# The last chunk of the first modulation weights, loaded as two halves on two DMA queues

## Chip, cores, metric

One core of one Trainium2 chip. The metric is device time in microseconds (us) of one execution. Beside it each execution has a span, from the first to the last instruction of the core, and the mean clock that TensorE was granted. The time is some 1.8 us longer than the span. The landing of a transfer is the moment at which the last of the 16 counts on its semaphore arrives; a ring is the part of a queue that one DMA engine works through.

## The reference, cut to what matters

```python
mod = (_silu(c) @ w_mod).reshape(c.shape[0], 6, 1, -1)       # c: 1 x 512, w_mod: 512 x 3072
sa, ca, ga, sb, cb, gb = (mod[:, 0].copy(), mod[:, 1].copy(), ...)   # cut: six rows of 512
h = _layernorm(x, axis=-1) * (1 + ca) + sa
x = x + ga * _A_ref(h, A_k_cache, A_v_cache, A_wq, A_wo)     # attention, 32 heads, window of 512 keys
h = _layernorm(x, axis=-1) * (1 + cb) + sb
x = x + gb * _B_ref(h, B_w1, B_w2)                           # two-layer relu network
```

Everything in attention needs h, and h needs sa (shift) and ca (scale), which are columns 0 to 1023 of w_mod. So the first 1 MB of w_mod, four chunks of 128 rows by 1024 columns, stands at the very head of the kernel.

## The kernel before

The chunks go alternately to ACT's and SP's queue, in 2 KB rows, each with a semaphore of its own:

```python
for i in range(2):     # x, first 512 rows, in two halves
    dma(x_sb[:, 2 * i:2 * i + 2, :], xv[:, 2 * i:2 * i + 2, :], f"xa{i}", ..., eng=ACT if i else SP)
dma(c_row[:, :], c[0].rearrange("(c p) -> c p", p=P), "c", writes=[R_c])
for i in range(DC):    # DC = 4
    load_wm01(i, (ACT, SP)[i % 2])
# cut: then on SP wq of the first two heads (two transfers), keys, wq, values

def mod_cols_mm(which, bk):                    # 32 matmuls of one column each
    for cc in range(DC):                       # chunk
        for sl in (0, 1):                      # shift half, scale half
            for c2 in range(DC):
                ...  mm(bank[bk][:, col:col + 1], wm[sl][:, cc, c2 * P:(c2 + 1) * P], sc_bf[:, cc:cc + 1], ...,
                        [R_sc, wm_res(sl, cc)], ...)     # waits for the chunk
```

On TensorE these 32 matmuls stand ahead of the transposes of normalised x (tile xn). VectorE then adds 1 to the scale (tile modc), and modc and the transposes make hT, with which the attention starts. Ahead of the 32, fifteen matmuls of ones keep TensorE busy so that it is granted its full clock.

Of the kernel before, what the change touches and what calls it, by code (L numbers as in the profile page):

```python
# [1198 lines left out]
def build_fast(nc, es, top, A_x, A_k_cache, A_v_cache, A_wq, A_wo, B_x, B_w1, B_w2, c, w_mod, out, flag):  # L1199
    P = 128  # L1200
    _, Sq, D = A_x.shape
# [10 lines left out]
    DC = D // P  # L1212
# [33 lines left out]
    wm01 = wmw[:, 0:2 * DC * D].rearrange("p (c n) -> p c n", c=DC)  # L1246
# [42 lines left out]
    ACT = kb.stream("act", sem("s_act"))  # L1289
    DVE = kb.stream("dve", sem("s_dve"))  # L1290
    POOL = kb.stream("pool", sem("s_pool"))
    SP = kb.stream("sp", sem("s_sp"))

    def dsem(key):
        if key not in kb.dma_cnt:
            kb.add_dma_sem(key, sem("d_" + key))
        return key

    def dma(out_ap, in_ap, key, reads=(), writes=(), transpose=False, eng=None):
        k = dsem(key)  # L1300
        if transpose:
            return kb.op(SP, lambda e: e.dma_start_transpose(out_ap, in_ap), reads=reads, writes=writes, dma_sem=k)
        return kb.op(eng or SP, lambda e: e.dma_start(out_ap, in_ap), reads=reads, writes=writes, dma_sem=k)  # L1303

    RL = lambda name, n: [Res(f"{name}{i}") for i in range(n)]
# [4 lines left out]
    R_acc, R_wm, R_w1, R_w2 = RL("acc", TPB), RL("wm", 6), RL("w1", FC), RL("w2", FC)  # L1310
# [6 lines left out]
    R_st, R_mv, R_rstd = RL("st", NT), RL("mv", NT), RL("rstd", NT)  # L1317
    R_h0 = RL("h0", DC)
    R_q1 = RL("q1_", 2)
    R_wmc = RL("wmc", DC)  # L1320
    R_wqa = RL("wqa", 2)
    R_nmr = Res("nmr")
    R_cf, R_m01 = Res("cf"), Res("m01")
# [27 lines left out]
    wm01v = w_mod[:, 0:2 * D].rearrange("(c p) n -> p c n", p=P)  # L1351

    def load_wm01(i, eng=None):
        dma(wm01[:, i, :], wm01v[:, i, :], f"wmc{i}", writes=[R_wmc[i]], eng=eng)

    def wm_res(sl, cc):
        return R_wmc[cc] if sl < 2 else R_wm[sl]

    def load_wo(j):
        dma(wo_sb[:, j * HQ:(j + 1) * HQ, :], wov[:, j * HQ:(j + 1) * HQ, :], f"wo{j}", writes=[R_wo[j]])  # L1360
# [66 lines left out]
    def mod_cols_mm(which, bk):  # L1427
        fs = []
        for cc in range(DC):
            for sl in (0, 1):  # L1430
                for c2 in range(DC):
                    last = sl == 1 and c2 == DC - 1 and cc == DC - 1
                    fs.append(lambda sl=sl, c2=c2, cc=cc, col=sl * DC + c2, last=last: mm(
                        bank[bk][:, col:col + 1], wm[sl][:, cc, c2 * P:(c2 + 1) * P], sc_bf[:, cc:cc + 1],
                        cc == 0 and sl == 0 and c2 == 0, last, [R_sc, wm_res(sl, cc)], [bk], last))
        return fs
# [130 lines left out]
    for i in range(DC):  # L1567
        load_wm01(i, (ACT, SP)[i % 2])
# [261 lines left out]
def bass_adaLN_cond__sliding_block_cached__dense_activation_relu__prompt_kernel(  # L1830
# [14 lines left out]
    with ExitStack() as top:  # L1845
        flag = top.enter_context(nc.sbuf_tensor("flag", [1, 8], mybir.dt.int32))
        with ExitStack() as es:
            kb, fast, cut, dma_cnt, flag_ev = build_fast(nc, es, top, *args, flag)
            sems = dict(kb.sems)
            meet = top.enter_context(nc.semaphore("s_meet"))  # L1850
# [84 lines left out]
```

## Time and profile before

| | before |
|---|---|
| time, median of 3 (560.13 to 560.22) | 560.16 us |
| span of the profiled execution | 559.0 us |
| TensorE busy | 553.9 us (99%) |
| chunk 3 in the chain of waits | 2.05 to 8.82 us |
| first hT written | 9.73 us |

The lines themselves stand in the prediction. They are to be read as one chain: only the head of the kernel waits for a transfer, everything after is TensorE's work.

### The profile page before, as it was taken

The page shows a single profiled execution, that of the slowest core. Times are in us where ns is not written, and L with a number is a line of the kernel's source. Part 1 is how long each engine was busy: PE and PEld are TensorE (multiplying, and loading weights), DVE is VectorE, ACT ScalarE, POOL GpSimd, SP SyncE. Part 2 cuts the span into 40 slices and gives each one's busy share as a digit, 9 for nine tenths or more (in the row PEclk, how much of TensorE's full clock was granted, in tenths as well). Part 3 has the DMA queues.
Part 4 walks back from the last instruction along what each step waited for, and adds up shares of the span by engine and source line. Part 5 has one row for each costly group of instructions (what it writes and reads, how often), then busy time and mean ns, then how long its engine had stood idle before and what let it go on. Part 6 is the DMA issues. An engine that isn't in the chain of part 4 may idle for free.

```text
span 559.0 us, 9759 instructions
## 1 busy us (share of the span) xinstructions
PE 553.9 (99%) x4139; PEld 316.6 (57%) x4139; DVE 254.9 (46%) x556; ACT 349.4 (63%) x455; POOL 52.7 (9%) x50
## 2 busy tenths in 40 slices
PE   8999999999999999999999999999999999999997
PEld 4665555555555555555555555555555554444444
DVE  5555555553546544335445443333354438322134
ACT  5986666666666666666666666666666644432500
POOL 2000022004400000033000000332000000000000
PEclk9999999999999999999999999999999999999999
DMA  9999763422224244353353312121123110200001
GB/s 234 296 196 185 136 166 42 114 43 73 38 41 74 39 84 106 61 130 58 96 95 57 76 40 39 39 38 38 39 39 76 39 29 0 50 28 21 21 29 48
DMA packets 113356, 42.66 MB, mean 76 GB/s; under 512 B 93976, under 2 KB 112152, under 8 KB 113304
## 3 DMA queue, kind: packets, MB, share of 16 engines
q1 hardware_dynamic: 112584, 41.08, 35.5%
q10 hardware_dynamic: 720, 0.89, 0.5%
q8 instruction: 33, 0.54, 0.4%
q14 instruction: 19, 0.16, 0.1%
HBM read 18.35 MB, written 2.10 MB: 37 GB/s over the span
## 4 chain that ended last, share of the span: by engine, by line
PE 98%; DMA 1%; SPq 0%; DVE 0%; issue 0%
PE psS L1374 29%; PE psO L1374 27%; PE psQ L1374 23%; PE psW L1374 20%; DMA wmw<-in_w_mod_dram 1%; SPq L1303 0%; PE psS L1377 0%; PE psO L1377 0%; DVE PT L1752 0%; DVE PT L1754 0%; PE psW L1377 0%
## 5 line engine op out<-in xcount | busy, mean ns | idle before, releaser
L1498 ACT ACTIVATE PT<-psS 128x1024 bf16<-128x1024 f32 x254 | 260.4, 1027 | 127.0 <-PE psS L1374 126.9
L1374 PE MATMUL psS<-qT,kT 128*128 128x512 bf16 (+1 forms) x516 | 151.8, 377 | 0.1
L1374 PEld LDWEIGHTS psO<-v,PT 128*128 128x128 bf16 x2048 | 126.6, 98 | 30.2
L1374 PE MATMUL psO<-v,PT 128*128 128x129 bf16 x2048 | 137.0, 220 | 0.0
L1374 PE MATMUL psW<-wo,oT 128*128 128x512 bf16 x512 | 130.6, 379 | 0.0
L1374 PE MATMUL psQ<-hT,wq 128*128 128x512 bf16 (+1 forms) x508 | 129.6, 377 | 0.0
L1508 DVE RECIPROCAL rinv<-psO 128x4 f32<-128x4 f32 x128 | 23.3, 182 | 225.3 <-PE psO L1374 225.3
L1509 DVE TENSOR_TENSOR o<-psO,rinv 128x512 bf16<-128x512 f32 x128 | 88.5, 691 | 4.7 <-DVE rinv L1508 0.3
L1374 PEld LDWEIGHTS psS<-qT,kT 128*128 128x128 bf16 x516 | 50.0, 98 | 58.7 <-issue 0.4
L1374 PEld LDWEIGHTS psQ<-hT,wq 128*128 128x128 bf16 x508 | 49.7, 98 | 59.0 <-ACT hT L1641 0.2
L1490 ACT ACTIVATE qT<-psQ 128x512 bf16<-128x512 f32 x125 | 73.9, 591 | 0.0
L1741 ACT ACTIVATE wq<-psS 128x512 bf16<-128x512 f32 x56 | 33.4, 597 | 49.1 <-PE psS L1374 49.1
L1374 PEld LDWEIGHTS psW<-wo,oT 128*128 128x128 bf16 x512 | 45.0, 98 | 32.9 <-DVE acc L1531 1.2
L1531 DVE TENSOR_TENSOR acc<-psW,acc 128x512 f32<-128x512 f32 x48 | 33.2, 691 | 6.7 <-PE psW L1374 6.7
L1374 PE MATMUL psO<-wmw,wq 128*128 128x512 bf16 (+1 forms) x168 | 32.9, 352 | 0.0
L1534 POOL TENSOR_TENSOR acc<-acc,gaf 128x512 f32<-128x512 f32 x12 | 15.6, 1301 | 146.9 <-DVE acc L1531 139.8
L1390 POOL TENSOR_TENSOR rstd<-rstd,cst 128x4 f32<-128x4 f32 x7 | 7.2, 1027 | 216.6 <-DVE rstd L1389 216.6
L1752 DVE TENSOR_TENSOR PT<-psO,gbf 128x512 f32<-128x512 f32 (+1 forms) x12 | 7.5, 624 | 40.4 <-PE psO L1374 40.4
L1374 PE MATMUL psS<-h2T,wmw 128*128 128x512 bf16 x112 | 25.3, 379 | 0.0
L1374 PEld LDWEIGHTS psO<-wmw,wq 128*128 128x128 bf16 x168 | 15.4, 98 | 16.5
L1374 PE MATMUL psS<-hT,wmw 128*128 128x512 bf16 x112 | 24.5, 379 | 0.0
L1384 DVE BATCH_NORM_STATS2 st<-x 128x6 f32<-128x512 bf16 x31 | 21.1, 680 | 3.7 <-DMA x<-in_A_x_dram 3.7
(93 smaller groups left out, 197.1 us busy)
## 6 DMA issues: line engine op xcount, KB each, us to landing
wo<-in_A_wo_dram SPq DMA_DIRECT2D x4, 1024.0 KB, 5.9
wq<-in_A_wq_dram SPq DMA_DIRECT2D x7, 512.0 KB, 4.5
wmw<-in_B_w_dram SPq DMA_DIRECT2D x14, 256.0 KB, 3.1
wmw<-in_w_mod_dram SPq DMA_DIRECT2D x4, 512.0 KB, 5.0
oT<-o SPq DMA_TRANSPOSE x128, 2.4
out_dram<-PT SPq DMA_DIRECT2D x15, 128.0 KB, 1.7
x<-in_A_x_dram SPq DMA_DIRECT2D x3, 512.0 KB, 4.3
v<-in_A_v_cache_dram SPq DMA_DIRECT2D x8, 128.0 KB, 4.5
```

The lines of the kernel that those rows point to most:

```text
L1374: kb.op(PE, lambda e: e.matmul(out_ap, lhsT, rhs, start=start, stop=stop), reads=reads, group_writes=[R_b[k] for k in bk], signal=signal)
L1384: kb.op(DVE, lambda e: e.bn_stats(st[:, t, :], x_sb[:, t, :]), reads=[R_x[t]], writes=[R_st[t]])
L1390: kb.op(POOL, lambda e: e.tensor_tensor(rstd[:, sl], rstd[:, sl], cst[:, 0:1].to_broadcast([P, hi - lo]), op=ALU.pow), reads=R_rstd[sl] + ...
L1490: kb.op(ACT, lambda e: e.activation(qT[u % NQT][:, :], bank[bk], ACTF.Copy), reads=[R_b[bk]], writes=[R_qT[u % NQT]])
L1498: kb.op(ACT, lambda e: e.activation(PT[u % NPT][:, pr * 2:pr * 2 + 2, :], s_ps[pr][:, :, :], ACTF.Exp, scale=scale), reads=[R_b[pr * 2], R ...
L1508: kb.op(DVE, lambda e: e.reciprocal(rinv[:, u, :], o_ps[:, :, P]), reads=[R_b[5], R_b[6]], writes=[R_rinv])
L1509: kb.op(DVE, lambda e: e.tensor_tensor(o_sb[u % NOS][:, :, :], o_ps[:, :, 0:P], rinv[:, u, :].unsqueeze(2).to_broadcast([P, TPB, P]), op=A ...
L1531: kb.op(DVE, lambda e: e.tensor_tensor(acc[:, tl, :], bank[WBK], acc[:, tl, :], op=ALU.add), reads=[R_b[WBK], R_acc[tl]], writes=[R_acc[tl]])
L1534: kb.op(eng, lambda e: e.tensor_tensor(acc[:, tl, :], acc[:, tl, :], gaf[:, :], op=ALU.mult), reads=[R_acc[tl], R_ga], writes=[R_acc[tl]])
L1741: kb.op(ACT, lambda e: e.activation(h1T[b % 2][:, fc, :], bank[bk], ACTF.Relu), reads=[R_b[bk]], writes=[R_h1[b % 2][fc]], pre=all_events( ...
L1752: kb.op(DVE, lambda e: e.tensor_tensor(yt[i][:, c0:c1], bank[bk][:, c0:c1], gbf[:, c0:c1], op=ALU.mult), reads=[R_b[bk], R_gb], writes=[R_ ...
```

## The change

Its intent: the last chunk is what the head waits for, and it comes late on SP's queue; half of it on each queue should arrive sooner. The shift columns go to ACT's queue, the scale columns to SP's, each half with its own semaphore.

```diff
-    R_wmc = RL("wmc", DC)
+    R_wmc = RL("wmc", DC + 1)
...
     def load_wm01(i, eng=None):
-        dma(wm01[:, i, :], wm01v[:, i, :], f"wmc{i}", writes=[R_wmc[i]], eng=eng)
+        if i < DC - 1:
+            dma(wm01[:, i, :], wm01v[:, i, :], f"wmc{i}", writes=[R_wmc[i]], eng=eng)
+        else:
+            for sl, eng in enumerate((ACT, SP)):
+                dma(wm01[:, i, sl * D:(sl + 1) * D], wm01v[:, i, sl * D:(sl + 1) * D], f"wmc{i + sl}", writes=[R_wmc[i + sl]], eng=eng)

     def wm_res(sl, cc):
-        return R_wmc[cc] if sl < 2 else R_wm[sl]
+        return R_wmc[cc + (sl if cc == DC - 1 else 0)] if sl < 2 else R_wm[sl]
```

## The prediction

> **What bounds the kernel now.** I read the page's chain first, then the same chain cut to the first 20 us, because the change touches only transfers that are issued in the first 3 us, then the instructions by time around the last wait, then the DMA part of the first 12 us, and last the records of single DMA packets. The page:
>
> ```profile
> PE 553.9 (99%) x4139; PEld 316.6 (57%) x4139; DVE 254.9 (46%) x556; ACT 349.4 (63%) x455; POOL 52.7 (9%) x50
> ...
> PE 98%; DMA 1%; SPq 0%; DVE 0%; issue 0%
> PE psS L1374 29%; PE psO L1374 27%; PE psQ L1374 23%; PE psW L1374 20%; DMA wmw<-in_w_mod_dram 1%; SPq L1303 0%; PE psS L1377 0%; PE psO L1377 0%; DVE PT L1752 0%; DVE PT L1754 0%; PE psW L1377 0%
> ```
>
> The kernel is bound by TensorE: of 559.0 us of span it is idle for 559.0 - 553.9 = 5.1 us, and the chain is 98% matmuls. The only transfer in the chain with a share worth printing is w_mod into tile wmw, 1%. No change to transfers can bring more than a few us of 560, so 2% (11.2 us) is out of reach upwards, and downwards it would need a new wait in the body of the kernel. The same chain over the first 20 us, in order of time (start, length, what):
>
> ```profile
> 1.65 0.36 SPq L1303
> 2.01 0.04 issue
> 2.05 6.77 DMA wmw<-in_w_mod_dram
> 8.82 0.05 issue
> 8.87 0.35 PE psQ L1374 x8
> 9.22 0.47 PE psS L1377 x8
> 9.69 0.43 PE psS L1374 x2
> ```
>
> This is the whole stake. The transfer issued at 2.05 us on the SP queue is chunk 3 of the weights (chunks 0 and 2 go on ACT's queue, 1 and 3 on SP's). It lands at 8.82 us; the eight small matmuls that use it follow, then the transposes, and from there PE work is contiguous. What chunk 3's landing moves, the end of the kernel moves, until another condition takes over. The instructions around it:
>
> ```profile
> 8.08 0.73 DVE L1395 TENSOR_SCALAR xn<-x,mv,rstd 128x512 bf16<-128x512 bf16 x2
> ...
> 8.10 0.47 PEld L1374 LDWEIGHTS psQ<-sc_bf,wmw 128*128 128x128 bf16 x16 [0.48 <-DMA wmw<-in_w_mod_dram]
> ...
> 8.86 0.27 PEld L1374 LDWEIGHTS psQ<-sc_bf,wmw 128*128 128x128 bf16 x8 [0.29 <-DMA wmw<-in_w_mod_dram]
> 8.87 0.35 PE L1374 MATMUL psQ<-sc_bf,wmw 128*128 128x1 bf16 x8 [0.21 <-DMA wmw<-in_w_mod_dram]
> ...
> 9.26 0.17 DVE L1440 TENSOR_TENSOR modc<-psQ,m 128x8 f32<-128x8 f32 x1 [0.45 <-PE psQ L1374]
> ```
>
> PE's matmul row idles only 0.21 us for chunk 3 itself, since chunks 1 and 2 arrived at about 8.1 and 8.2 us. It also shows how much could ever be won: the second tile of xn, which the next transposes need, is ready at 8.08 + 0.73 = 8.81 us. With chunk 3 at hand at 8.1 us, the transposes of that tile would start at 8.81 instead of about 9.3 us, so the ceiling of the gain is about 0.5 us.
>
> The DMA part of the first 12 us gives sizes and time from issue to landing:
>
> ```profile
> wmw<-in_w_mod_dram ACTq DMA_DIRECT2D x2, 256.0 KB, 5.4
> wmw<-in_w_mod_dram SPq DMA_DIRECT2D x2, 256.0 KB, 6.6
> ...
> wq<-in_A_wq_dram SPq DMA_DIRECT2D x2, 128.0 KB, 6.7
> ```
>
> SP's chunks take 1.2 us longer, which invites the change: ACT's queue looks less loaded. The packet records say more. The landing of each chunk is counted from 16 engines. For chunk 3, fifteen of these arrive by about 7.9 us and the last at 8.82; for chunk 1 fifteen by 6.65 and the last at 8.06. So one lagging engine sets the wait. (The records don't name the engine; I infer it from packets that start where the last one ended.) On it, 2 KB packets follow each other every 80 to 84 ns. ACT's ring ends chunk 2 there at 7.84 us, SP's ring has ended chunk 1 at 7.67 us, then the eight packets of chunk 3 run alone and end at 7.92, 8.00, 8.08, ... 8.48 us; the semaphore is seen 0.34 us later, at 8.82.
>
> **What the Trainium skill says.** "DMA: Bandwidth & Descriptors", section "Issuing engines are not separate DMA queues": transfers started by different engines end on the same 16 DMA engines and interleave, and only issue time on the sequencer is saved. The trace agrees: on the lagging engine the pitch is 80 to 84 ns whether one ring or both have work. Same page, "Queues, rings and completion order": each engine takes turns between the rings that have work. The trace agrees, SP's and ACT's 2 KB packets alternate there until 7.8 us. Same page, "Why a DMA increments its semaphore by 16 and not by 1": a wait is for all engines used, which is why the laggard counts. Nothing else that I use rests on a page.
>
> **The change, part by part.** Rows of chunk 3 are 1024 bf16, 2 KB; each half has rows of 1 KB. Removed: one 256 KB transfer on SP, 128 packets of 2 KB, eight per engine. Added: 128 KB on ACT's queue behind chunk 2 (shift columns) and 128 KB on SP's behind chunk 1 (scale columns), 256 packets of 1 KB, sixteen per engine.
> - Bytes before the end of chunk 3: the same 1.5 MB (x 512 KB, weights 1 MB) for both queues together. SP had 256 + 256 + 256 = 768 KB, ACT had the same 768 KB. The rings were even in bytes; the split gives ACT 896 and SP 640.
> - Packets: over the whole trace the median is 84 ns for 2 KB, 46 ns for 1 KB and 27 ns for 512 B. On the lagging engine chunk 3 then costs 16 x 46 = 736 ns instead of 8 x 81 = 648 ns (7.84 to 8.48): **+0.09 us**. Where 1 KB rows of wq were loaded alone at 11 to 13 us, 32 packets per engine took 1.73 us, 54 ns each, which would make it 864 ns, +0.22 us.
> - Turns: SP's ring is about two packets ahead there (7.67 against 7.84 us), so its half ends first and the 512 B packets of wq behind it take turns with the last one to three packets of ACT's half: 2 x 27 ns, **+0.05 us**.
> - Issue: ACT's queue issues one more, about 0.45 us (its two issues took 0.94 us together), starting at about 2.2 us. The activation table load moves from 2.20 to about 2.65 us; ACT idles 1.26 us before x arrives at 4.96, so this costs 0. The half on ACT is issued some 0.1 us after the half on SP; both are long before 7.8 us, so 0.
> - Matmuls: the same 32. The four shift matmuls of chunk 3 come first in program order and wait for ACT's half. If it lands last, all eight still follow it (0.35 us). If it lands first, four lie ahead of the wait, and about 0.1 us is saved. I expect ACT's half last: 0.
> - Behind it: wq for the first two heads moves little and has landed by about 9.7 us against a use at 10.4; k0 lands at about 10.3 against a use at 11.65; later transfers have more. No new wait.
> Sum: +0.09 to +0.22, plus 0.05, middle about **+0.2 us** on chunk 3's landing, carried to the end by the contiguous PE chain: 560.16 + 0.2 = about 560.3 us.
>
> **Rivals.** (1) The intended gain: ACT's ring has slack and both halves land 0.3 to 0.5 us earlier, 559.7 to 559.9 us. For it: ACT's chunks land 1.2 us sooner after issue, and on the fifteen quick engines ACT's ring is done while SP's still has much of chunk 3. Against it: the wait needs the slow engine, where the rings end chunks 1 and 2 within 0.17 us of each other and the engine is busy without a gap. (2) Fair sharing hurts more: SP's ring finishes its half early and the 256 KB of wq compete with ACT's half. If that held fully on the slow engine, as many bytes again as chunk 3 would stand ahead, 8 x 81 ns = 0.65 us: 560.8 us. Against it: there the rings are nearly level. (3) The laggard's stalls shift. Its 48 packets of 2 KB would need 48 x 83 = 4.0 us of the 6.4 us from 2.1 to 8.5, so some 2.4 us are stalls (some packets took 400 to 750 ns) whose cause I can't read. More or fewer of them move the time by 0.5 us either way, limited below by the 0.5 us ceiling. (4) A new wait in the body, for instance for wq or the keys: the slack above speaks against it; it would be 1 us at most.
>
> **Range and chances.** Rivals 1 and 2 bracket the sum: 559.7 to 560.9 us should hold it 8 times in 10. The three runs before spread 0.09 us, so noise adds little. All rivals together are below 0.3% of the time, far inside 2%; I leave 0.5% for each side beyond.
>
> **What would show it.** Right: the transfer at the head of the chain ends at 8.9 to 9.1 us, on ACT's queue; the eight matmuls follow at about 9.1; all later groups keep their counts and means. Wrong: the chunk lands before 8.7 us (rival 1), or after 9.3 us with wq landing ahead of it (rival 2), or the laggard's chunks 1 and 2, which the change leaves alone, land elsewhere than at 8.06 and 8.24 us (rival 3), or PE idles for wq or keys after 10 us (rival 4).

## The result, and the profile after

The changed kernel took 560.33 us (median of 6, 560.12 to 562.37), the kernel before 560.23 us (median of 6, 560.13 to 560.43). The ratio is 1.0007, 95% interval 0.9993 to 1.0021: the same. (A ratio is the mean time of one kernel's fast runs over that of the other's of the same rounds, so it is not quite the ratio of the medians.) The time lies on the prediction. It tests little, though: the kernel before, with medians of 560.07 to 560.36 us in its four sets of executions, lies in the predicted range too.

The profiled execution is the slowest of the six, 562.37 us. From the page of the changed kernel, its busy time and the granted clock in 40 slices:

```profile
PE 555.2 (99%) x4139; PEld 317.5 (57%) x4139; DVE 255.1 (46%) x556; ACT 349.7 (62%) x455; POOL 52.7 (9%) x50
...
PEclk8999999999999999999999999999999999999999
```

TensorE has the same 4139 matmuls and is busy 1.3 us longer; the first slice has an 8 where the kernel before has a 9. The chain of the changed kernel in its first 13 us, in order of time (start, length, what):

```profile
1.72 0.45 ACTq L1303
2.17 0.03 issue
2.20 6.49 DMA wmw<-in_w_mod_dram
8.69 0.05 issue
8.73 0.35 PE psQ L1378 x8
9.09 0.88 PE psS L1381 x8
9.96 0.85 PE psS L1378 x2
```

As predicted, the transfer at the head is now ACT's half of chunk 3. But it lands at 8.69 us, 0.13 us sooner than chunk 3 did before, and not at the predicted 8.9 to 9.1 us. What is worse comes after it: the eight transposes take 0.88 us instead of 0.47, the two matmuls after them 0.85 instead of 0.43. Busy time by stretch shows why (columns: stretch and length, busy us of each engine with counts, granted TensorE clock, DMA share, GB/s):

```profile
5.54:8.95 3.41, 2.64 (x40) 1.32 (x40) 2.98 (x12) 2.13 (x8) 2.04 (x4) 1.00 1.25 235
8.95:12.36 3.41, 3.41 (x29) 2.61 (x26) 1.87 (x7) 1.67 (x4) 0.00 (x0) 0.50 1.12 271
```

From 8.95 to 12.36 us TensorE ran at half clock (half clock means that the trace shows TensorE granted half its full clock). That, and not a transfer, made this one execution 2 us slower than the other five. It is recorded as a mean clock of 0.997; the five others have 0.999 or 1.000. So there are two things to explain: what the split does when the clock is full, and whether the split brings the half clock.

The DMA part of the first 12 us (size, then us from issue to landing) shows the two halves level:

```profile
wmw<-in_w_mod_dram ACTq DMA_DIRECT2D x2, 256.0 KB, 5.1
...
wmw<-in_w_mod_dram SPq DMA_DIRECT2D x1, 256.0 KB, 6.0
...
wmw<-in_w_mod_dram SPq DMA_DIRECT2D x1, 128.0 KB, 6.5
wmw<-in_w_mod_dram ACTq DMA_DIRECT2D x1, 128.0 KB, 6.5
```

Each half, with half the bytes, takes as long from issue to landing as the whole chunk's 6.77 us before, within 0.3 us.

### The profile page after: what moved, and what is told of

Read it like the earlier page. It is cut to its first block, busy times and chain, and to the rows that moved or that the text cites. A ratio compares the mean times of both kernels' runs of the same rounds, so it can differ in the third digit from the quotient of the medians.

```text
span 560.5 us, 9760 instructions
## 1 busy us (share of the span) xinstructions
PE 555.2 (99%) x4139; PEld 317.5 (57%) x4139; DVE 255.1 (46%) x556; ACT 349.7 (62%) x455; POOL 52.7 (9%) x50
## 4 chain that ended last, share of the span: by engine, by line
PE 98%; DMA 1%; ACTq 0%; DVE 0%; issue 0%
PE psS L1378 29%; PE psO L1378 27%; PE psQ L1378 23%; PE psW L1378 20%; DMA wmw<-in_w_mod_dram 1%; ACTq L1303 0%; PE psS L1381 0%; PE psO L1381 0%; DVE PT L1756 0%; DVE PT L1758 0%; PE psW L1381 0%
```

## The experiments

Theory A: both queues share the DMA engines, and the split moves chunk 3's landing by a tenth or two of a us. Its rival, the queue theory: ACT's queue has room that SP's lacks. Clock theory: the half-clock stretch follows a stretch in which TensorE did too little, and depends on the phase at which the clock is granted. Its rivals: it is chance alone, or the split's own cost.

Twelve kernels were run, each with six executions on a chip, beside executions of the kernel before (11 on the first chip, 12 on the second). All gave correct results, apart from the one kernel that was expected to be wrong: its error is within the tolerance. I count an execution as half clock if its mean clock is 0.997, and take the mean span of the others:

| kernel | median us | ratio, 95% interval | mean span at full clock (n) | half clock |
|---|---|---|---|---|
| before, chip 1 / chip 2 | 560.20 / 560.36 | | 558.47 (10) / 558.48 (9) | 1 of 11 / 3 of 12 |
| split, first measurement | 560.33 | 1.0007, 0.9993 to 1.0021 | 558.50 (5) | 1 of 6 |
| e1 split again (chip 1) | 560.08 | 1.0002, 0.9985 to 1.0019 | 558.20 (5) | 1 of 6 |
| e2 before again (chip 1) | 560.07 | 0.9993, 0.9981 to 1.0006 | 558.30 (6) | 0 of 6 |
| e3 halves both on SP (chip 1) | 560.20 | 0.9996, 0.9983 to 1.0008 | 558.40 (6) | 0 of 6 |
| e4 chunk 3 whole on ACT (chip 1) | 561.72 | 1.0018, 1.0001 to 1.0035 | 558.80 (3) | 3 of 6 |
| e5 chunk 3 not awaited (chip 2) | 560.40 | 0.9996, 0.9981 to 1.0011 | 558.33 (6) | 0 of 6 |
| e6 256 KB more ahead of it (chip 2) | 561.62 | 1.0015, 0.9995 to 1.0036 | 558.60 (3) | 3 of 6 |
| e7 split by partitions (chip 2) | 560.64 | 1.0005, 0.9988 to 1.0022 | 558.74 (5) | 1 of 6 |
| e8 split, queues exchanged (chip 2) | 560.41 | 0.9998, 0.9981 to 1.0015 | 558.44 (5) | 1 of 6 |
| e9 before, filled (chip 2) | 561.64 | 1.0016, 1.0001 to 1.0031 | 558.60 (6) | 0 of 6 |
| e10 as e4, filled (chip 2) | 562.09 | 1.0023, 1.0007 to 1.0038 | 558.93 (6) | 0 of 6 |
| e11 split, filled (chip 2) | 561.55 | 1.0014, 0.9998 to 1.0030 | 558.47 (6) | 0 of 6 |
| e12 as e6, filled (chip 2) | 562.19 | 1.0023, 1.0008 to 1.0038 | 559.07 (6) | 0 of 6 |

"Filled" is explained at e9. A single full-clock span of the kernel before ranges from 558.1 to 559.3 us, so differences of 0.2 us between two rows are at the edge of what these runs resolve.

**e1, the split again.** No edit.

> The changed kernel once more, unaltered. The profiled execution of the first measurement took 562.37 us, the other five 560.12 to 560.65; its trace shows TensorE's clock at half for one stretch of 3.4 us (8.95 to 12.36 us). Theory A (transfers share the engines; what the split does is a tenth or two of a us at the landing of chunk 3): median 560.2 to 560.5 us, ratio 0.9995 to 1.0010, chunk 3 lands 0.6 to 0.9 us after chunk 2. Clock theory: most executions near 560.3, and about one in six over 561.5 us, with half clock after 8 us in the trace if the profile catches one. Rival (the split itself costs 1.5 us or more): the profile shows a span of 560 us or more again with full clock.

The ratio is 1.0002, five executions took 560.00 to 560.11 us and one 562.32 us at clock 0.997, so the clock theory's one in six came out, and the split itself does not cost 1.5 us. Its profile is at full clock: the chain at the head reads

```profile
2.21 5.81 DMA wmw<-in_w_mod_dram
8.02 0.05 issue
8.06 0.35 PE psQ L1378 x8
8.41 0.54 PE psS L1381 x8
```

Chunk 3 landed at 8.02 us, 0.50 us after chunk 2, where theory A expected 0.6 to 0.9: a miss to the good side. Its transposes began earlier, but waited inside for xn (0.54 instead of 0.47 us).

**e2, the kernel before again.** No edit.

> The kernel before, unaltered, as the noise floor of both the time and the trace. All theories: ratio 0.9995 to 1.0005. Theory A: chunk 2 lands between 7.7 and 8.3 us, and chunk 3 0.5 to 0.65 us after it, wherever the lagging engine stands. Clock theory: if the half-clock stretch is a matter of phase alone, the kernel before has it too in some executions (over 561.5 us); if it is the change that opens the gap, never.

Chunk 2 landed at 8.03 us and chunk 3 at 8.55, 0.53 us after, as expected. The ratio is 0.9993, just outside the expected band: the noise floor is some 0.07%, 0.4 us. None of its six executions was at half clock, but one of the 11 executions of the kernel before beside it was (562.14 us), and three of 12 on the other chip. So the half clock is not the split's own; the split had it in 2 of 12, the kernel before in 4 of 35 (all executions together). These do not differ.

**e3, both halves on SP's queue.**

```diff
-            for sl, eng in enumerate((ACT, SP)):
+            for sl, eng in enumerate((SP, SP)):
```

> Chunk 3 in two halves of 1 KB rows, but both on SP's queue. It separates the size of the packets from the second queue. Theory A: on the slowest engine the same 16 packets of 1 KB, nothing beside them; chunk 3 lands 0.6 to 0.85 us after chunk 2, time 560.2 to 560.5 us, as the split over both queues within 0.15 us. Queue theory (ACT's ring has room that SP's has not): later than the split over both queues by 0.3 us or more.

Its last half landed 0.50 us after chunk 2 (7.72 against 7.22 us), not 0.6 to 0.85, and the time is the kernel before's. The queue theory's 0.3 us of loss did not come. The trace tells less than hoped: in this execution no engine lagged, chunk 1 was down at 6.20 us where the other profiles have 7.0 to 8.1.

**e4, chunk 3 whole on ACT's queue.**

```diff
-        load_wm01(i, (ACT, SP)[i % 2])
+        load_wm01(i, (ACT, SP, ACT, ACT)[i])
```

> Chunk 3 whole, 2 KB rows, on ACT's queue behind chunk 2; SP's next transfer is wq. Theory A: the rings are level on the slowest engine, so chunk 3 stays eight packets, but wq's 512 B packets take turns with it: landing 0.65 to 0.95 us after chunk 2, time 560.2 to 560.6 us. Queue theory: ACT's ring is ahead, so chunk 3 lands 0.3 us earlier than in the kernel before, 559.8 us.

Chunk 3 landed 0.93 us after chunk 2 (9.10 against 8.18), in theory A's band, and the full-clock spans are 0.33 us longer than those of the kernel before on the same chip. The queue theory, 0.3 us of gain, is refuted: on the engine that counts, chunk 3 did not end sooner on ACT's queue. (Only three executions stand behind the 0.33 us; the pair e10 and e9 below, six each, gives 0.33 us again.) Three of six executions were at half clock, so the median rose to 561.72 us, which neither theory of the transfers foresaw.

**e5, chunk 3 not awaited** (wrong: chunk 3 is not loaded, chunk 2 stands in for it).

```diff
-    for i in range(DC):
+    for i in range(DC - 1):
         load_wm01(i, (ACT, SP)[i % 2])
...
-   wm[sl][:, cc, ...] ... [R_sc, wm_res(sl, cc)]
+   wm[sl][:, min(cc, DC - 2), ...] ... [R_sc, wm_res(sl, min(cc, DC - 2))]
```

> Wrong result on purpose: chunk 3 is not loaded, and its 32 small products are taken from chunk 2's weights, so that the wait is gone and 256 KB as well. It measures the whole stake. Theory A: the start wins at most what the next condition leaves, about 0.5 us (the second tile of xn is ready at 8.8 us): 559.6 to 559.9 us. Rival (the start of the kernel does not carry to the end): 560.1 to 560.3 us. A larger win, under 559.5, would show that the next condition was misjudged.

The time is 560.40 us; the expected 559.6 to 559.9 did not come. By span the gain is 0.15 us (558.33 against 558.48), and in this kernel the time outside the span is 0.2 us longer than in the others (2.0 to 2.1 instead of 1.7 to 2.0), which I cannot explain. The chain of its profile:

```profile
1.65 6.09 DMA wmw<-in_w_mod_dram
7.75 0.05 issue
7.79 0.75 PE psQ L1374 x24
8.54 0.64 PE psS L1377 x8
9.19 0.43 PE psS L1374 x2
```

The transposes now take 0.64 instead of 0.47 us: they wait inside for the second tile of xn, ready at 8.73 us. That is the next condition, as predicted, but in most executions it stands closer than the 0.5 us that I read from one: the profiled execution of the kernel before, 559.0 us, was itself 0.5 us longer than the mean span of 558.47 us. All 12 full-clock profiles follow one rule. The first hT is written 0.91 us after the last chunk's landing, or 0.49 us after the second xn, whichever is later:

| profile | last chunk lands | second xn | rule | first hT |
|---|---|---|---|---|
| before | 8.82 | 8.81 | 9.73 | 9.73 |
| e2 before again | 8.55 | 8.60 | 9.46 | 9.46 |
| e1 split | 8.02 | 8.51 | 9.00 | 9.00 |
| e3 | 7.72 | 8.78 | 9.27 | 9.27 |
| e5 | 7.94 (chunk 2) | 8.73 | 9.22 | 9.22 |
| e7 | 8.65 | 8.64 | 9.56 | 9.56 |
| e8 | 8.60 | 8.73 | 9.51 | 9.41 |
| e12 | 9.10 | 8.73 | 10.01 | 10.00 |

The four that are not listed agree within 0.01 us: e6 10.08, e9 9.55, e10 9.78 and e11 9.55 us.

What happens at the head does reach the end: from the start of the first values matmul to the end of the span it is 542.8 to 543.0 us in these profiles (before 559.0 - 16.0, e1 558.1 - 15.3, e5 558.3 - 15.5). The stake is small because the two conditions stand side by side, and because the last landing itself moves from execution to execution.

**e6, 256 KB more on SP's queue ahead of chunk 3.**

```diff
+        if i == DC - 1:
+            dma(PT[2][:, 0:2, :].rearrange("p a b -> p (a b)"), wm01v[:, 0, :], "extra", writes=[R_PT[2][0]], eng=SP)
         load_wm01(i, (ACT, SP)[i % 2])
```

> The kernel before with another 256 KB of 2 KB rows on SP's queue just ahead of chunk 3 (into a buffer that is free then). Theory A: eight more packets of 81 to 84 ns on the slowest engine stand before the end of chunk 3: landing 1.15 to 1.3 us after chunk 2, time 560.8 to 561.0 us, carried one to one. If ACT's ring has room that SP's lacks, the cost is SP's alone and the same; this run is for the size of the term and for the carry. Clock theory: a longer idle stretch of TensorE makes the half clock likelier, more executions over 561.5 us.

Chunk 3 landed 0.80 us after chunk 2, less than the 1.15 to 1.3 expected: on the slow engine chunk 2 was itself late here (8.38 us; chunk 1 at 7.29), so part of the extra rows ran beside it. Against the kernel before, chunk 3 came at 9.18 instead of 8.82 and 8.55 us. The half clock came in three of six, as the clock theory expected of a longer idle stretch; the median, 561.62 us, is that. The other three took 560.14, 560.15 and 561.06 us, with a mean span only 0.12 us above the kernel before, so the expected 560.8 to 561.0 us, carried one to one, was missed as well.

**e7, split by partitions, 64 on each queue, so that packets stay 2 KB.**

```diff
-dma(wm01[:, i, sl * D:(sl + 1) * D], wm01v[:, i, sl * D:(sl + 1) * D], ...)
+dma(wm01[sl * 64:(sl + 1) * 64, i, :], wm01v[sl * 64:(sl + 1) * 64, i, :], ...)
```
(and each product of chunk 3 waits for both halves)

> Chunk 3 split over both queues by partitions (64 each) instead of by columns, so that the packets stay 2 KB. Theory A (size of packets): eight packets of 2 KB on each engine again, 0.55 to 0.7 us after chunk 2, time as the kernel before within 0.15 us and 0.05 to 0.2 us below the split by columns. Rival (turns with wq cost as much as the packet size): no better than the split by columns.

Chunk 3 landed 0.58 us after chunk 2, as expected. The full-clock spans are 558.74 us, 0.26 above the kernel before (0.15 was allowed) and not below the split by columns: the expected gain did not appear, and the packet size is not worth a version.

**e8, the split with the queues exchanged.**

```diff
-            for sl, eng in enumerate((ACT, SP)):
+            for sl, eng in enumerate((SP, ACT)):
```

> The split by columns with the queues exchanged: the shift half, which the matmuls use first, on SP's queue, the scale half on ACT's. Theory A: the half on ACT lands last, as in the changed kernel; four of the eight matmuls of chunk 3 now run before the last wait, which wins about 0.1 to 0.15 us: the last matmul of psQ ends 0.2 us after the last landing instead of 0.35 us. Rival (the last landing decides alone): same as the changed kernel within 0.05 us.

ACT's half lands last again (8.60 against 8.23 us), and modc starts 0.34 us after it instead of 0.44 (9.26 - 8.82 before): four of the eight products ran ahead of the last wait. The 0.10 us is the one line of the table above that beats the rule. In the spans (558.44 us) it cannot be told from noise.

**e9 to e12, filled.** Three more matmuls of ones in TensorE's idle stretches, in four kernels: before (e9), e4 (e10), the split (e11), e6 (e12).

```diff
-    for f in fs:
-        f()
+    for i, f in enumerate(fs):      # the 32 products
+        f()
+        if i in (7, 23):
+            warm(2 if i == 7 else 1)
```

> The kernel before with three more 512-column matmuls of ones (results unused), two between the products of chunks 0 and 1 and one between those of chunks 2 and 3, where TensorE idled for 0.4 to 0.5 and 0.2 to 0.5 us. Clock theory (a half-clock stretch of 3.4 us follows a stretch in which TensorE did too little): no execution at granted clock 0.997, against 3 of 34 executions of the kernel before so far; full-clock executions unchanged within 0.15 us. Phase-only rival: the half clock stays as likely as before, 1 in 12.

> The same three matmuls in the kernel with chunk 3 whole on ACT's queue, which had the half clock in 3 of 6 executions. Clock theory: 0 or 1 of 6, and the median falls from 561.7 to about 560.6 us. Rival (the half clock comes with the longer wait by another way, such as the transfers themselves): 2 to 4 of 6 again.

> The same three matmuls in the split kernel, which had the half clock in 2 of 12 executions. Clock theory: 0 of 6, full-clock spans 558.2 to 558.5 us, level with the kernel before filled within 0.2 us. Rival: 1 or more of 6 at half clock.

> The same three matmuls in the kernel with 256 KB ahead of chunk 3, which had the half clock in 3 of 6 executions. Clock theory: 0 or 1 of 6, the full-clock spans stay at 558.3 to 559.2 us. In the trace the rule of two conditions holds again: the first hT starts 0.91 us after the last chunk's landing or 0.49 us after the second tile of xn is ready, whichever is later, within 0.1 us. Rival: 2 to 4 of 6 again.

None of the 24 executions was at half clock. The strongest pair is e4 and e6 against e10 and e12: 6 of 12 before the filling, 0 of 12 with it. (e4 ran on the first chip and e10 on the second; e6 and e12 ran on the same one.) Busy time by stretch, first in e4 and then in e10, whose phases of the clock are 0.42 us apart:

```profile
5.84:9.25 3.41, 2.34 (x33) 1.10 (x34) 2.77 (x11) 2.04 (x7) 2.05 (x4) 1.00 1.22 218
9.25:12.66 3.41, 3.19 (x29) 2.67 (x30) 1.74 (x6) 1.55 (x3) 0.00 (x0) 0.50 1.12 275
```

```profile
5.42:8.83 3.41, 3.08 (x34) 1.32 (x33) 3.14 (x13) 2.13 (x9) 2.00 (x4) 1.00 1.19 238
8.83:12.24 3.41, 3.19 (x39) 2.42 (x40) 2.25 (x7) 2.56 (x7) 0.05 (x1) 1.00 1.10 268
```

Where TensorE was busy 2.34 us of the 3.41 us, the next 3.41 us were at half clock; with 3.08 us they were not. The split's two profiles show the same: 2.64 us in the first measurement, and in e1

```profile
5.45:8.86 3.41, 3.11 (x47) 1.90 (x48) 3.20 (x13) 2.21 (x7) 2.04 (x4) 1.00 1.14 246
```

So far the clock theory stands: with TensorE's idle stretches filled, the half clock was gone. How little work is too little, the busy time of the matmul row does not tell. In e6 full clock was first granted at 6.96 us, and the next two stretches read

```profile
6.96:10.37 3.41, 2.51 (x46) 1.82 (x45) 2.53 (x10) 1.26 (x3) 1.88 (x4) 1.00 1.20 237
10.37:13.78 3.41, 3.28 (x32) 2.42 (x31) 2.18 (x7) 2.96 (x7) 0.00 (x0) 1.00 1.19 295
```

That is less busy than the split's 2.64 us, and the clock stayed full; e8, busy 2.58 us from 3.89 us on, kept it too. If only the matmuls of more than eight columns are added up in the same traces, the two stretches before a half clock have 1.32 us (e4) and 1.42 us (the split), and the first stretch after the grant in the other 12 profiles has 1.57 us (e6) to 2.86 us (e9). That orders all 14, but by a margin of 0.15 us and with two half-clock profiles; no run was made to test it.

By the Trainium skill, "TensorE: Matmul & The Clock Gate", section "Part 1: The HAM clock gate (the "warmup" mystery)", activity is watched in free-running windows of 3413 ns, and the clock is full or half. The traces agree: the half-clock stretches at the head are 3.41 us long, and full clock was first granted between 3.89 and 6.96 us in the profiles. In the two half-clock profiles it came at 5.54 and 5.83 us, so that the window that follows holds the waits for the chunks. The phase does not decide alone: in e1 and e3 it came at 5.45 and 5.56 us, but the chunks landed sooner, TensorE was busy for 3.11 and 2.92 us, and the clock stayed full.

The filled kernels are no improvement, though. Their spans are about level with the unfilled ones (e9 558.60 against 558.48), but the time outside the span rose from 1.7 to 2.0 us to 2.7 to 3.5 us, in all 24 executions. The traces' clock records go on for 3.2 to 3.7 us after the last instruction, against 2.2 in the kernel before. So three more matmuls cost some 1 us after the end of the work. The profile does not show what it is, and I leave it open. Without a remedy for it, no version beats both kernels. The split filled (558.47 us) and before filled (558.60 us) are level within 0.2 us, as expected, and e10 and e12 are 0.33 and 0.47 us longer than e9, the sign and order that theory A has for them. In e12 chunk 3 landed 1.27 us after chunk 2, which is the term that e6 had missed.

## Why the prediction was right, point by point

The number came out, and so did the conclusion that the split does not matter much. The path to the number did not. By the prediction's own signs it was wrong: the last half landed at 8.69 us (and at 8.02, 8.60 and 8.64 us in e1, e8 and e11), sooner than the 8.7 us that it named as a sign of rival 1, and chunks 1 and 2 landed at 7.68 and 7.84 us instead of 8.06 and 8.24, its sign of rival 3. A cost of 0.2 us is also small beside the spread of single full-clock spans, 558.1 to 559.3 us. That 560.3 us came out so exactly is luck.

**The bound and its consequence** held: 4139 matmuls, 99% busy, and only the head could move.

**What invited the change**, that SP's chunks take 1.2 us longer from issue to landing, is a misreading of medians of two. Chunk 0, the first on ACT's queue, took 4.22 us and pulls ACT's figure down. Chunk 2 on ACT's queue took 6.53 us and chunk 1 on SP's 6.41 us: no difference in favour of ACT's.

**The term of chunk 3**, about +0.2 us, is not shown: three split profiles have it in sum but not in its parts, and a fourth does not have it. On the slowest engine one can take the time from the last 2 KB packet of chunk 2 (or, where chunks 1 and 2 end together, the last on ACT's ring) to chunk 3's last packet, and from there to the landing:

| | to the last packet of chunk 3 | from there to the landing | sum |
|---|---|---|---|
| whole: before, e2, e9 | 0.646, 0.646, 0.646 | 0.34, 0.32, 0.36 | 0.99, 0.96, 1.01 |
| split: first, e1, e11 | 0.742, 0.694, 0.689 | 0.49, 0.41, 0.54 | 1.23, 1.10, 1.23 |
| split, queues exchanged: e8 | 0.576 | 0.37 | 0.95 |

The sums of the first two rows differ by 0.20 us in the mean. But e8 sends packets of the same sizes over the same two queues, only with the columns exchanged, and its sum is not above that of the whole chunk. With it the difference is 0.14 us, half of the 0.28 us by which the split's own four sums vary. In the first two rows, packets and turns together make 0.06 of it, not 0.14 to 0.27: 1 KB packets follow each other every 42 ns on that engine, half of 80 to 84, so the 46 or 54 ns a packet that I took was too much. The other 0.14 us is a term that the prediction did not have: the landing follows the last packet later. The Trainium skill, "DMA: Bandwidth & Descriptors", section "Queues, rings and completion order", offers a reason: the write to the semaphore lands only after every earlier write of that engine, across its queues, and in the split SP's ring is already moving wq beside ACT's half. No run here shows that this is it. With wq moving beside ACT's part of chunk 3 the landing came 0.39 us after the last packet in e4 and e10, 0.37 in e8 and 0.55 in e7; with all of chunk 3 on SP's ring and ACT's ring done, 0.36 in e6, 0.42 in e12 and 0.56 in e3.

**Carried to the end, 560.3 us:** the number is right, and the step to it is not shown. In the first three split profiles the slowest engine was done with chunk 2 earlier, at 7.46, 6.92 and 7.41 us against 7.84, 7.59 and 7.64. So the last landing was on average no later but 0.2 us earlier (8.69, 8.02, 8.64 against 8.82, 8.55, 8.64). This is rival 3, the moving stalls, at its predicted size. Whether the split causes it or three executions against three fell that way stays open. The full-clock spans of the split (558.50, 558.20, filled 558.47) lie on both sides of those of the kernel before (558.47, 558.48, 558.30, filled 558.60): neither +0.2 nor the intended gain is resolved. What is shown is that the effect is below about 0.3 us.

**The ceiling of 0.5 us** was too high as a general figure. It was read from one execution in which chunk 3 was late; without the wait at all (e5) the spans gain 0.15 us.

**Rival 1** (ACT's queue has room) fell with e4. **Rival 2** (sharing with wq) has a size in e4 and e10: 0.33 us of span when all of chunk 3 stands beside wq.

**The parts that should cost nothing** cost nothing: the table load of activations moved from 2.20 to 2.69 us, and ACT still idled 0.69 us for x; wq of the first heads and the first keys landed at 9.41 and 10.01 us (9.74 and 10.30 before), and no new wait appeared.

**Not foreseen:** the half clock. It costs about 2 us, ten times the whole effect, in 4 of 35 executions of the kernel before and 2 of 12 of the split, and grows to 3 of 6 where chunk 3 comes later.

## What to carry to other kernels

A second queue brought nothing here, where the wait was for the slowest of the shared engines: look at the last landings and at the packets there before splitting a transfer. Before valuing a wait from one profile, look for the condition that stands next to it, and take a second profile: in the kernel before and the split, the start that each allows lay within 0.5 us of the other's, now one later and now the other. And a short wait at the head can cost more through the clock that TensorE is granted afterwards than through its own length, so list the granted clock of every execution before comparing medians.

## What the Trainium skill lacked or had wrong

- "TensorE: Matmul & The Clock Gate", section "HAM oscillation — how this bites in real kernels", gives as its abstract rule that TensorE should have no idle gaps over about 3.4 us. Here the clock fell to half after a stretch in which no idle gap of the matmul row was over 0.6 us and the row counted as busy for 2.34 to 2.64 of 3.41 us, 28 and 32 of its matmuls having one column only. Busy share alone is no better rule: after 2.51 us (e6) and 2.58 us (e8) the clock did not fall. Counting only matmuls of more than eight columns orders these runs (1.32 and 1.42 us before a half clock, 1.57 us and more otherwise). The page's next section does tell of short idles between groups of matmuls that make the clock swing, but gives no size for them.
- "DMA: Bandwidth & Descriptors" says, in the section cited above, that a semaphore's write waits for earlier writes of its engine across queues, but gives no size. Here the landing of chunk 3 came 0.32 to 0.56 us after the last packet on the slowest engine, and a second ring at work does not sort these figures (0.37 to 0.55 us with it, 0.32 to 0.56 us without).
- No page that I read says how far one engine can lag behind the others on loads from SP's and ACT's queues (the page on DMA names two engines as usually slower, without a size, and suspects another kind of queue as the reason): chunk 1's last of 16 arrivals came 1.4 us after the fifteenth in the kernel before (8.06 against 6.65 us), and under 0.3 us after it in e3.
- No page that I read explains why three matmuls more should cost 1 us after the last instruction (2.7 to 3.5 us outside the span in 24 executions, against 1.7 to 2.0).
